# A transform-and-MLP kernel: the transforms end 16 ticks sooner, and one more block of tokens takes the seven-product form

## The chip, the cores and the metric

The kernel runs on one core of a Trainium2 chip. The metric is the device time of one execution in microseconds, given as the median of several runs. Its five engines appear as PE (TensorE matmuls; PEld is its weight load), DVE (VectorE), ACT (ScalarE), POOL (GpSimd) and SP (SyncE, which here only issues DMAs).

## What is computed

```python
# x: 4 x 3008 x 256
X = np.fft.rfft(x, axis=1)
Yr = Xr @ w_r - Xi @ w_i + b_r
Yi = Xr @ w_i + Xi @ w_r + b_i
Yr = np.sign(Yr) * np.maximum(np.abs(Yr) - 0.01, 0.0)     # Yi likewise
y = np.fft.irfft(Yr + 1j * Yi, n=3008, axis=1)
h = y.reshape(12032, 256) @ w_in                          # 2048 wide
out = (h * (1.0 / (1.0 + np.exp(-h)))) @ w_out            # 256 wide
```

A Fourier transform along the sequence, a complex 256 x 256 product with soft thresholding, the inverse transform, and then an MLP with SiLU over 12032 tokens. Matrices are kept as a high and a low part, so a product is three matmuls.

## The kernel before

The MLP is the frame. Its 12032 tokens are 24 blocks of 512 (the last has 256), and each block takes 16 **ticks**, one for each 128 of the 2048 hidden columns. In a plain tick t TensorE does six matmuls of 512 columns (`mlp1`, line 599), then what the table `fill` holds for that tick, then four pairs of accumulating matmuls (`mlp2`, lines 757 and 761) for the hidden columns of two ticks ago, then what `fill` holds for t + 0.5. ScalarE does SiLU and the rounding to the high part (lines 606, 615), VectorE the low part (line 616). Blocks 10 to 22, the set `FAST`, compute the first product in the seven-product form of Strassen and Winograd: for two ticks 21 matmuls of 256 columns (`fast_product`, line 680) instead of 12 of 512, with sums of the moving matrix on GpSimd (`fast_moving`) and sums of the products on VectorE (`fast_more`, `fast_two`). The weights' sums (`fast_weights`) and buffers for this need the memory that the transforms hold, so `swap_pools` frees it after the last transform step.

The transforms of batches 1 to 3 stand in `fill`, tick by tick. (Batch 0 and the first stage of batch 1 run ahead of tick 0.) Each has
- 16 **pieces** of the first stage for batches 2 and 3: `stack_split` splits an input tile into high and low (ScalarE line 283, VectorE line 284) two ticks or so ahead of `stack_product` (two matmuls, line 293), whose results ScalarE and VectorE add (lines 294, 295). The tile comes by a DMA from GpSimd's queue.
- 15 **steps** (`u3_step(b, u, 0)`): the second stage for pair u of frequencies (`s2_3`: eight matmuls, line 390; ScalarE lines 398, 399, 401; VectorE lines 400, 402, 403), the split of an earlier result into zh and zl (`split_z`, lines 447, 448), and the inverse for a still earlier one (`i1`: six matmuls, line 462, copied by ScalarE in line 466 and stored).
- 12 **mixes** (`u3_step(b, u, 1)`, `mix3`): three products of six matmuls (line 415). The first is copied to q by ScalarE (line 421), and GpSimd adds the biases to it (lines 422, 423). The other two fill the two halves of a second bank, which VectorE adds to q in the deferred `shrink` (line 434, four times; then lines 437 and 438 for the threshold). `shrink` is issued ahead of the next tick or half tick.

Steps, mixes and pieces take their banks of PSUM by turns from two (`bank`), so each takes the bank that the last but one used and waits for its readers. `i2` and `i2_ends` (lines 524, 531) turn a block into the MLP's layout, at half ticks where a tick already has work.

The order comes from a planner loop in the last part of the kernel. It goes through the ticks from 24 on, gives each at most one of piece, mix and step, leaves out the first tick of a block (`boundary`), and adds the turnings that are due. In before it ends at tick 148, in block 9.

Of the kernel before, what the change touches and what calls it, by code (L numbers as in the profile page):

```python
# [33 lines left out]

STACKED = 2

FAST = range(10, 23)

X_BUFS = [0, 1, 2, 3, 4, 5, 6, 0, 1, 2, 3, 4, 0, 2, 1, 0]
BLOCKS = [(c, min(BLK, NT - c)) for c in range(0, NT, BLK)]  # L40
# [109 lines left out]
def spectral_mlp_kernel(ctx: ExitStack, tc: tile.TileContext, x, w_r, w_i, b_r, b_i, w_in, w_out, c1, c2, c3, c4, c3f, c5, out):  # L150
    nc = tc.nc
# [8 lines left out]
    x_sb = [tf.tile([128, 4 * D], F32, name=f"x_sb{i}") for i in range(2)]  # L160
    c4_sb = cst.tile([120, 2 * (NP + RR)], F32, name="c4_sb")
    c5_sb = tf.tile([128, 128], F32R, name="c5_sb")
# [9 lines left out]
    state = {"prologue": True, "fast": False, "d": 0, "xy": 0}  # L172
    tl = None

    def bank(name):

        state["d"] += 1
        tag, bufs = f"d{state['d'] % 2}", 1
        if state["prologue"]:
            tag, bufs = ((f"d{state['d'] // 4 % 2}", 1), ("acc", 4), ("h", 2), ("acc", 4))[state["d"] % 4]  # L180
        if state["fast"]:
            tag = "d1"
        return ps.tile([128, 512], F32, tag=tag, bufs=bufs, name=name)
# [30 lines left out]

    def x_load_twice(b, q):

        t = x_sb[q % 2]
        if b == STACKED and q < 2:
            nc.gpsimd.memset(t[32:64, :], 0.0)
        h, g = divmod(q, 8)  # L220
        v = x[b].rearrange("(n h j) d -> n h (j d)", h=2, j=NJ)[:, h, g * 4 * D:(g + 1) * 4 * D]
        for p in (0, 64):
            nc.gpsimd.dma_start(out=t[p:p + RR, :], in_=v)
        return t
# [143 lines left out]
    def mix3_weights():  # L368
        t = tf.tile([128, 2, 2 * D], F32, tag="s1o", bufs=2, name="w32")
        nc.sync.dma_start(out=t[:, :, 0:D], in_=w_r.rearrange("(e p) d -> p e d", p=128))  # L370
        nc.sync.dma_start(out=t[:, :, D:2 * D], in_=w_i.rearrange("(e p) d -> p e d", p=128))
        for i, v in enumerate((b_r, b_i)):
            nc.sync.dma_start(out=bias[:, i, :], in_=v.unsqueeze(0).to_broadcast([128, D]))
        yield
        ds = []
        for op in (ALU.subtract, ALU.add):
            ds.append(tf.tile([128, 2, D], F32, tag="i1o", bufs=2, name="w32d"))
            nc.vector.tensor_tensor(out=ds[-1], in0=t[:, :, D:2 * D], in1=t[:, :, 0:D], op=op)
        yield
        for d, dst in zip(ds, (wi, ws)):  # L380
            nc.scalar.copy(dst[0], d)
            nc.vector.tensor_sub(dst[1], d, dst[0])
# [95 lines left out]
    def pieces(c0, n):  # L478

        c = c0  # L480
        while c < c0 + n:
            b, q = divmod(c, S)
            v = next(v for v in PLACES[b] if v[0] <= q < v[0] + v[1])
            p0 = q - v[0]
            m = min(v[1] - p0, c0 + n - c)
            yield c - c0, b, v, p0, m
            c += m
# [47 lines left out]

    def stage_bank(name, i):

        if i < 3 or state["fast"]:
            return bank(name)
        return ps.tile([128, 512], F32, tag="h", bufs=2, name=name)  # L540

    def i2(i, e):

        c0, n = BLOCKS[i]
        if e == 0:
            v = "ab"[i > 0] if i < 3 else "ab"[(i + 1) % 2]
            xt[i] = tuple(sb.tile([128, 2, BLK], F32R, tag=f"xt{v}{k}", bufs=1, name=f"xt{k}") for k in range(2))
        whole = [v for v in pieces(c0, n) if v[4] == v[2][1]]
        p = stage_bank("i2", i)
        for o, b, place, _, m in whole:  # L550
            i2_columns(p[:, o:o + m], e, b, place)
        q = slice(whole[0][0], whole[-1][0] + whole[-1][4])
        if i in FAST and e == 0:
            xf[i] = tl.tile([128, 2, BLK], F32, tag="xf", bufs=1, name="xf")
        split_x(i, p[:, q], (slice(None), e, q))

    def split_x(i, v, q):
        h, l = xt[i]
        nc.scalar.copy(h[q], v)
        if i in FAST:  # L560
            nc.scalar.copy(xf[i][q], v)
# [59 lines left out]
    xf, th, tw, fast = {}, {}, {}, []  # L621
# [118 lines left out]
    def mlp2(i, f, t):  # L740
# [31 lines left out]
        if i == LAST:  # L772
            (nc.vector.tensor_copy if t % 2 else nc.scalar.copy)(out=o, in_=a[:, 0:D])
        elif i in FAST and t < 2:
            w = sb.tile([128, 512], F32, tag="g", bufs=3, name="ow")
# [72 lines left out]
    with tc.manual_schedule():  # L848
# [156 lines left out]
        def at(t, fn, *args):  # L1005
            fill.setdefault(t, []).append((fn, args))

        taken = {9, 25} | set(range(33, len(ticks), NFF))

        def put(t, fn, *args):  # L1010

            while t in taken:
                t += 1
            taken.add(t)
            at(t, fn, *args)
            return t

        def last_stage(i, first):

            at(first - 2, i2_load, i)  # L1020
            put(first, i2, i, 0)
            put(first + 2, i2, i, 1)
            at(first + 2, i2_load, i, True)
            return put(first + 4, i2_ends, i)

        for k, fn in enumerate(((i2, 1, 0), (i2, 1, 1), (i2_ends, 1))):
            put(1 + 2 * k, *fn)
        last_stage(2, 25)
        for t, n in enumerate(W_GO):
            at(t, w_go, n)  # L1030
        at(0, x_ahead)
        for i in range(2):
            put(5, s1_later, 7, i)
        for t in (11, 35):
            at(t, x_ahead)
        at(30, nc.gpsimd.dma_start, c5_sb, c5)
        m3 = mix3_weights()
        for t in (16, 22, 23):
            at(t, next, m3, None)
# [1 line left out]
        steps = []  # L1041
# [2 lines left out]
                steps.extend((b, u, half) for half in range(2 if 0 < u <= NU else 1))  # L1044
        pieces_left = [(b, q) for b in range(STACKED, NB) for q in range(16)]
        turned = []
        for i in range(3, FAST[0]):
            at(16 * i - 15, i2_load, i)
            begins = any(v[1] and v[2][0] == 0 for v in pieces(*BLOCKS[i]))
            turned.extend((16 * i - (3 if k == 2 and begins else 13), 16 * i - 7 + 2 * k, fn)  # L1050
                          for k, fn in enumerate(((i2, i, 0), (i2, i, 1), (i2_ends, i))))
        stacked, last, begun = {1: 18}, 24, set()
        ended = {}
        done, t, since = 37, 24, 0
        while steps or turned:
            boundary = t % NFF == 1 and t > 32
            stage = None
            if not boundary and t not in taken:
                b = steps[0][0] if steps else NB
                ready = b in stacked and t >= stacked[b] + (4 if b > 1 else 0)  # L1060
                apart = 2 + (ready and b > 1 and len(pieces_left) % 2)
                if pieces_left and t >= done + apart and pieces_left[0][0] <= b + 1:
                    stage = "piece"
                elif ready:
                    stage = "mix" if steps[0][2] else "step"
            more = None
            if turned and t >= turned[0][0] and t >= since + 2 and not (boundary and t < turned[0][1]):
                if stage in ("mix", None) or t >= turned[0][1]:
                    more = turned.pop(0)[2]
                    since = t  # L1070
            if stage == "piece":
                at(max(t - 2, done), stack_split, *pieces_left[0])
                at(t, stack_product, *pieces_left[0])
                done = t
                if pieces_left.pop(0)[1] == 15:
                    stacked[max(stacked) + 1] = t
            elif stage:
                if b not in begun:
                    begun.add(b)
                    for k in range(2):  # L1080
                        at(t - 2 + k, u_load, b, k)
                at(t, u3_step, *steps.pop(0))
                last = t
                ended[b] = t
            if more:
                at(t + 0.5 * (stage is not None), *more)
                if more[0] is i2_ends:
                    at(t - 2, i2_load, more[1], True)
            t += 1
        assert ended[1] < 16 * 5 - 5 and ended[2] < 16 * 11 - 15 and ended[3] < 16 * 17 - 15  # L1090
        assert all(16 * i > t for t, v in fill.items() for fn, (i, *_) in [(v[0][0], v[0][1] or (99,))] if fn is i2_ends)

        for i in range(FAST[0], len(BLOCKS)):
            if i in FAST:
                first = max(16 * i - 13, last + 1)
                t = last_stage(i, first)
# [13 lines left out]
        for q in range(NFF // 2):  # L1110
            steps = fast_weights(q)
# [20 lines left out]
        for t in range(len(ticks) + 1):  # L1132
            i, f = ticks[t] if t < len(ticks) else (LAST, None)
# [4 lines left out]
            if i in FAST:  # L1138
                q = t - first_fast
# [62 lines left out]
```

## Time and profile before

| | |
|---|---|
| median of 3 runs | 1337.1 us (1334.11 to 1339.39) |
| profiled execution | 1336.09 us |
| its span | 1334.2 us |
| TensorE busy | 1320.7 us (99%), 8437 matmuls |
| VectorE, ScalarE, GpSimd busy | 907.5 (68%), 811.4 (61%), 215.0 (16%) us |
| chain that ended last | PE 93%, DMA 3%, DVE 1%, ACT 1% |

The busy time of matmuls is a union of modelled spans, which overlap: a matmul of 512 columns is shown with about 396 ns and one of 256 with 281 ns, but in a row they start closer together. What a matmul costs TensorE is read from the starts in the timeline. The chain follows the work that ended last back from the end of the program; it runs almost wholly through TensorE. The MLP's lines 757, 680, 599 and 761 hold 73% of it.

### The profile page before, as it was taken

To read this page: it belongs to the slowest core of one execution; us is meant where nothing else is said; L and a number is where in the kernel's file an instruction comes from. 1 tells how busy PE (TensorE), PEld (TensorE's weight loads), DVE (VectorE), ACT (ScalarE), POOL (GpSimd) and SP (SyncE) were. 2 spreads that over 40 slices of the span, in tenths; PEclk is the share of its full clock that TensorE was granted. 3 is DMA by queue.
4 is the path that set the end of the run, shared out by engine and by line. 5 is a ranking of instruction groups with operands and counts; after the bars stand their busy time and mean duration, and the time that the engine had idled before them with its cause. 6 is when DMAs were issued, how large, how long until landed. Compare 5 with 4: busy or idle time off the path is not lost.

```text
span 1334.2 us, 22834 instructions
## 1 busy us (share of the span) xinstructions
PE 1320.7 (99%) x8437; PEld 1182.2 (89%) x8437; DVE 907.5 (68%) x1742; ACT 811.4 (61%) x1712; POOL 215.0 (16%) x322
## 2 busy tenths in 40 slices
PE   8999999999999999999999999999999999999998
PEld 4977888888888888889988999999999999999998
DVE  3767747877767777566658766666666666666663
ACT  5546555766767666555455666566656665666555
POOL 2001002222212122111202111121112111211100
PEclk9999999999999999999999999999999999999999
DMA  8875414454455443424220111011001110110000
GB/s 267 267 218 185 142 55 116 107 153 114 120 149 142 123 139 93 121 79 124 77 69 3 45 32 29 3 32 32 21 3 46 32 32 2 32 31 14 3 23 25
DMA packets 76124, 110.00 MB, mean 82 GB/s; under 512 B 8854, under 2 KB 54798, under 8 KB 76014
## 3 DMA queue, kind: packets, MB, share of 16 engines
q1 hardware_dynamic: 61895, 79.17, 20.4%
q0 software_dynamic: 10544, 25.68, 7.6%
q10 hardware_dynamic: 3575, 3.70, 0.9%
q8 instruction: 67, 1.10, 0.3%
q14 instruction: 43, 0.35, 0.1%
HBM read 71.03 MB, written 37.49 MB: 81 GB/s over the span
## 4 chain that ended last, share of the span: by engine, by line
PE 93%; DMA 3%; DVE 1%; ACT 1%; issue 0%; SPq 0%; POOL 0%; ACTq 0%; DVEq 0%
PE acc L757 25%; PE h L680 19%; PE h L599 16%; PE acc L761 13%; PE mix L415 6%; PE s L390 2%; PE i L462 2%; PE mix L354 2%; PE i L531 2%; PE i2e L531 2%; PE s L293 1%; DMA scr<-i1o 1%; DMA scr<-s1o 1%; PE acc L752 1%; PE i L459 1%; PE s L333 1%
## 5 line engine op out<-in xcount | busy, mean ns | idle before, releaser
L757 PE MATMUL acc<-wout,gh 128*128 128x512 f32 x1472 | 539.8, 396 | 0.6 <-ACT gh L615 0.6
L761 PE MATMUL acc<-wout,gl 128*128 128x256 f32 x1472 | 413.6, 281 | 0.5 <-DVE gl L616 0.5
L757 PEld LDWEIGHTS acc<-wout,gh 128*128 128x128 f32 x1472 | 277.9, 189 | 48.5 <-ACT gh L615 0.8
L761 PEld LDWEIGHTS acc<-wout,gl 128*128 128x128 f32 x1472 | 277.1, 188 | 4.9 <-DVE gl L616 1.6
L599 PE MATMUL h<-xt,win 128*128 128x512 f32 (+1 forms) x1056 | 265.9, 387 | 0.0
L599 PEld LDWEIGHTS h<-xt,win 128*128 128x128 f32 x1056 | 181.4, 188 | 36.1 <-DVE xt L563 0.4
L606 ACT ACTIVATE g<-h 128x512 f32<-128x512 f32 (+1 forms) x177 | 102.1, 577 | 134.2 <-PE h L599 132.2
L728 DVE TENSOR_TENSOR gl<-gp,gh 128x512 fp32r<-128x512 f32 x208 | 148.5, 714 | 31.8 <-ACT gh L727 31.8
L718 ACT ACTIVATE gp<-gp 128x256 f32<-128x256 f32 x104 | 43.4, 417 | 176.8 <-DVE gp L715 176.8
L616 DVE TENSOR_TENSOR gl<-g,gh 128x512 fp32r<-128x512 f32 (+1 forms) x177 | 117.5, 664 | 49.1 <-ACT gh L615 47.6
L727 ACT CAST gh<-gp 128x512 fp32r<-128x512 f32 x208 | 128.9, 620 | 6.6
L680 PE MATMUL h<-xt,win 128*128 128x256 f32 x624 | 108.9, 283 | 0.2 <-DVE gp L715 0.2
L615 ACT CAST gh<-g 128x512 fp32r<-128x512 f32 (+1 forms) x177 | 106.1, 600 | 1.0
L720 DVE TENSOR_TENSOR gp<-h,u 128x256 f32<-128x256 f32 x104 | 44.2, 425 | 78.8 <-ACT gp L719 78.8
L680 PEld LDWEIGHTS h<-xt,win 128*128 128x128 f32 x624 | 88.6, 189 | 5.1 <-DVE gp L715 0.7
L434 DVE TENSOR_TENSOR y<-q,mix 64x256 f32<-64x256 f32 x144 | 60.3, 419 | 46.9 <-PE mix L415 41.2
L680 PE MATMUL h<-th,sw_h 128*128 128x256 f32 x312 | 91.3, 292 | 0.0
L680 PE MATMUL h<-th,sw_l 128*128 128x256 f32 x312 | 88.4, 283 | 0.0
L680 PE MATMUL h<-tl,sw_h 128*128 128x256 f32 x312 | 87.7, 281 | 0.0
L422 POOL TENSOR_TENSOR q<-q,bias 128x256 f32<-128x256 f32 x36 | 28.1, 780 | 356.3 <-ACT q L421 356.3
L715 DVE TENSOR_TENSOR gp<-h,u 128x256 f32<-128x256 f32 x104 | 44.1, 424 | 54.8 <-PE h L680 54.5
L726 ACT ACTIVATE gp<-gp 128x512 f32<-128x512 f32 x104 | 66.4, 639 | 0.0
(175 smaller groups left out, 2431.6 us busy)
## 6 DMA issues: line engine op xcount, KB each, us to landing
a<-scr SPq DMA_DIRECT2D x48, 256.0 KB
x_sb<-in_x_dram POOLq DMA_DIRECT2D x64, 188.0 KB, 3.7
gin<-scr SPq DMA_DIRECT2D x48, 192.0 KB
t<-in_c_dram POOLq DMA_DIRECT2D x36, 256.0 KB, 3.5
scr<-i1o SPq DMA_DIRECT2D x36, 256.0 KB
t<-in_c_dram SPq DMA_DIRECT2D x48, 128.0 KB
scr<-s1o SPq DMA_DIRECT2D x32, 192.0 KB
scr<-s1o SPq DMA_DIRECT2D x13, 384.0 KB
```

What stands on the lines that cost most here:

```text
L415: nc.tensor.matmul(out=out, lhsT=x_[:, e, c, :], rhs=m[:, e, :], start=(n == 0), stop=(n == 5))
L434: nc.vector.tensor_tensor(out=y[64 * i:64 * i + 64, r, :], in0=q[rows, i, :], in1=pv[rows, i, :], op=op,)
L599: nc.tensor.matmul(out=p[:, :n], lhsT=w[:, e, f * 128:(f + 1) * 128], rhs=v[:, e, :n], start=(m == 0), stop=(m == 5),)
L606: nc.scalar.activation(out=g[:, q], in_=p[:, q], func=ACTF.Silu)
L615: nc.scalar.copy(gh[:, q], g[:, q])
L616: nc.vector.tensor_sub(gl[:, q], g[:, q], gh[:, q])
L680: nc.tensor.matmul(out=p, lhsT=w[j], rhs=m[k], start=(begins and n == 0), stop=(n == 2), skip_group_check=True,)
L726: nc.scalar.activation(out=v, in_=v, func=ACTF.Silu)
L727: nc.scalar.copy(h, v)
L728: nc.vector.tensor_sub(l, v, h)
L757: nc.tensor.matmul(out=a, lhsT=gh[:, q], rhs=wout[:, f].rearrange("p a c -> p (a c)"), start=begins, stop=False,)
L761: nc.tensor.matmul(out=a[:, D:2 * D], lhsT=gl[:, q], rhs=wout[:, f, 0, :], start=False, stop=ends,)
```

## The change

Block 9 joins `FAST`, so the transforms have to be done and the pools swapped ahead of it, 16 ticks sooner. To that end the planner's rules are altered: pieces of batch 2 start at tick 26 instead of 39, one every fourth tick at first (the first three share one input buffer, since the other holds half an output of block 0 until tick 33); block 2's turning goes by the planner; and a mix may share its tick with the step behind it, which then stands at t + 0.5. That is so for 14 ticks: 63, 64, 66 (batch 1), 72, 85, 96 (batch 2), 115, 116, 119, 120, 123, 124, 127 and 128 (batch 3). The last steps stand at ticks 67, 109 and 132 (before: 73, 119 and 148).

```diff
-FAST = range(10, 23)
+FAST = range(9, 23)
 ...
-        t = x_sb[q % 2]
-        if b == STACKED and q < 2:
+        t = x_sb[0 if b == STACKED and q < 3 else q % 2]
+        if b == STACKED and q in (0, 3):
             nc.gpsimd.memset(t[32:64, :], 0.0)
 ...
-        if i < 3 or state["fast"]:
+        if i < 2 or state["fast"]:
             return bank(name)
         return ps.tile([128, 512], F32, tag="h", bufs=2, name=name)
 ...
-        last_stage(2, 25)
+        at(23, i2_load, 2)
+        at(24, i2_load, 2, True)
 ...
-        for t in (11, 35):
+        for t in (11, 36):
             at(t, x_ahead)
-        at(30, nc.gpsimd.dma_start, c5_sb, c5)
+        at(12, nc.gpsimd.dma_start, c5_sb, c5)
 ...
-        for i in range(3, FAST[0]):
-            at(16 * i - 15, i2_load, i)
+        for i in range(2, FAST[0]):
+            if i > 2:
+                at(16 * i - 15, i2_load, i)
             begins = any(v[1] and v[2][0] == 0 for v in pieces(*BLOCKS[i]))
-            turned.extend((16 * i - (3 if k == 2 and begins else 13), 16 * i - 7 + 2 * k, fn)
+            turned.extend((25 if i == 2 else 16 * i - (3 if k == 2 and begins else 13), 16 * i - 7 + 2 * k, fn)
                           for k, fn in enumerate(((i2, i, 0), (i2, i, 1), (i2_ends, i))))
 ...
-        done, t, since = 37, 24, 0
+        done, t, since = 22, 24, 0
         while steps or turned:
             boundary = t % NFF == 1 and t > 32
             stage = None
-            if not boundary and t not in taken:
+            double = False
+            if (not boundary or steps and steps[0][2]) and t not in taken:
 ...
-                if pieces_left and t >= done + apart and pieces_left[0][0] <= b + 1:
+                if not boundary and pieces_left and t >= (done + 4 if len(pieces_left) > 29 else max(38 * (len(pieces_left) == 29), done + apart)) and pieces_left[0][0] <= b + 1:
                     stage = "piece"
                 elif ready:
                     stage = "mix" if steps[0][2] else "step"
+                    double = stage == "mix" and not boundary and len(steps) > 1 and (b == 3 and steps[0][1] % 3 or b == 2 and steps[0][1] % 4 == 1 or b == 1 and 2 in stacked)
 ...
-                if stage in ("mix", None) or t >= turned[0][1]:
+                if stage in ("mix", None) and not double or t >= turned[0][1]:
 ...
                 at(t, u3_step, *steps.pop(0))
+                if double:
+                    at(t + 0.5, u3_step, *steps.pop(0))
 ...
             if more:
                 at(t + 0.5 * (stage is not None), *more)
-                if more[0] is i2_ends:
+                if more[0] is i2_ends and more[1] > 2:
                     at(t - 2, i2_load, more[1], True)
```

The first place is VectorE at the end of batch 1. In before it does, from the last mix of the batch (tick 71) on: the sums and threshold of `shrink` (lines 434, 437, 438), a turning (line 563), the MLP's split (616), zl (448), and then the split of an input piece (284).

```order
L616 TENSOR_TENSOR gl<-g,gh 128x512
L434 TENSOR_TENSOR y<-q,mix 64x256 x4
L437 TENSOR_SCALAR q<-y 128x512
L438 TENSOR_TENSOR y<-y,q 128x512
L563 TENSOR_TENSOR xt_3767<-i_3935,xt_3766 128x376
L616 TENSOR_TENSOR gl<-g,gh 128x512
L448 TENSOR_TENSOR zl<-y,zh 128x512
L284 TENSOR_TENSOR sx<-x_sb_72,sx 47x1024
```

The same place now, from the block's output sums (line 780, tick 65) on:

```order
L780 TENSOR_TENSOR o<-acc,o 128x256 x4
L616 TENSOR_TENSOR gl<-g,gh 128x512
L284 TENSOR_TENSOR sx<-x_sb_72,sx 47x1024
L434 TENSOR_TENSOR y<-q,mix 64x256 x4
L437 TENSOR_SCALAR q<-y 128x512
L438 TENSOR_TENSOR y<-y,q 128x512
L448 TENSOR_TENSOR zl<-y,zh 128x512
```

The split of the input piece moved ahead of the sums, and zl follows the threshold with nothing between.

The second place is ScalarE in batch 3, one mix (copy of q, line 421) with the step behind it and the next mix. In before the step has a tick of its own, so the MLP's cast and SiLU of that tick (615, 606) stand between q and the step's xh (398), here with a turning (559) too:

```order
L421 COPY q<-mix 128x256
L559 CAST xt_6778<-i_6780 128x235
L615 CAST gh<-g 128x512
L606 ACTIVATE g<-h 128x512
L398 CAST xh<-s_6804 128x2x256
L399 COPY xs<-s_6804 128x256
L401 CAST xh<-xs 128x2x128
L447 CAST zh<-y 128x512
L466 COPY i1o<-i_6822 128x512
L615 CAST gh<-g 128x512
L606 ACTIVATE g<-h 128x512
L421 COPY q<-mix 128x256
```

The same place now, at a doubled tick (119 and 120):

```order
L421 COPY q<-mix 128x256
L398 CAST xh<-s_6423 128x2x256
L399 COPY xs<-s_6423 128x256
L401 CAST xh<-xs 128x2x128
L447 CAST zh<-y 128x512
L466 COPY i1o<-i_6441 128x512
L615 CAST gh<-g 128x512
L606 ACTIVATE g<-h 128x512
L421 COPY q<-mix 128x256
```

Between two mixes the work of one tick, one cast and one SiLU, has gone; on TensorE that is one `mlp1` and one `mlp2`.

## Rows read from the trace of the kernel before

**Rows 1.** The page's first part: span; busy us of each engine, share, instructions.
```profile
span 1334.2 us, 22834 instructions
PE 1320.7 (99%) x8437; PEld 1182.2 (89%) x8437; DVE 907.5 (68%) x1742; ACT 811.4 (61%) x1712; POOL 215.0 (16%) x322
```

**Rows 2.** Windows: length, busy us of PE, PEld, DVE, ACT, POOL; PEclk, DMA, GB/s.
```profile
175.00:727.00 552.00, 551.60 (x3286) 486.71 (x3285) 394.18 (x714) 342.12 (x680) 112.78 (x177) 1.00 0.40 108
727.00:1304.00 577.00, 576.81 (x4059) 540.08 (x4058) 389.37 (x811) 358.10 (x811) 89.83 (x120) 1.00 0.09 24
```

**Rows 3.** Timeline of TensorE, two plain ticks: start, us, engine, line, operation.
```profile
604.05 1.57 PE L599 MATMUL h<-xt,win 128*128 128x512 f32 x6
...
606.86 1.55 PE L599 MATMUL h<-xt,win 128*128 128x512 f32 x6
```

**Rows 4.** Timeline of TensorE, two pairs of ticks of a fast block.
```profile
900.04 0.53 PE L680 MATMUL h<-xt,win 128*128 128x256 f32 x3
...
905.36 0.53 PE L680 MATMUL h<-xt,win 128*128 128x256 f32 x3
```

**Rows 5.** Timeline of TensorE: a step, a plain tick's work, a mix.
```profile
618.08 1.05 PE L390 MATMUL s<-t,a 128*128 128x128 f32 x8
618.88 0.36 PE L462 MATMUL i<-zh,t 128*128 128x256 f32 x1
...
619.68 0.40 PE L757 MATMUL acc<-wout,gh 128*128 128x512 f32 x1
...
621.08 1.56 PE L599 MATMUL h<-xt,win 128*128 128x512 f32 x6
622.48 0.40 PE L415 MATMUL mix<-wr,xh 128*128 128x256 f32 x2
...
624.51 0.28 PE L415 MATMUL mix<-ws,xl 128*128 128x256 f32 x1
```

**Rows 6.** Timeline of ScalarE behind the step of rows 5.
```profile
620.83 0.62 ACT L447 CAST zh<-y 128x512 fp32r<-128x512 f32 x1
621.35 0.58 ACT L466 COPY i1o<-i 128x512 f32<-128x512 f32 x1
```

**Rows 7.** Timeline of VectorE behind the step and the mix of rows 5.
```profile
620.40 0.68 DVE L402 TENSOR_TENSOR xl<-s,xh 128x512 fp32r<-128x512 f32 x1
...
621.48 0.69 DVE L448 TENSOR_TENSOR zl<-y,zh 128x512 fp32r<-128x512 f32 x1
...
624.90 1.72 DVE L434 TENSOR_TENSOR y<-q,mix 64x256 f32<-64x256 f32 x4 [1.73 <-PE mix L415]
```

**Rows 8.** Timelines of TensorE and VectorE: a mix and a split in one tick.
```profile
229.99 0.28 PE L415 MATMUL mix<-ws,xl 128*128 128x256 f32 x1
...
230.27 1.74 DVE L284 TENSOR_TENSOR sx<-x_sb,sx 47x1024 fp32r<-47x1024 f32 x1 [1.63 <-ACT sx L283]
232.04 1.72 DVE L434 TENSOR_TENSOR y<-q,mix 64x256 f32<-64x256 f32 x4
...
234.26 0.69 DVE L438 TENSOR_TENSOR y<-y,q 128x512 f32<-128x512 f32 x1
```

**Rows 9.** Timelines of TensorE, ScalarE and VectorE: a mix whose q is late.
```profile
393.97 0.28 PE L415 MATMUL mix<-ws,xl 128*128 128x256 f32 x1
...
393.72 0.38 ACT L421 COPY q<-mix 128x256 f32<-128x256 f32 x1
...
394.95 1.72 DVE L434 TENSOR_TENSOR y<-q,mix 64x256 f32<-64x256 f32 x4 [0.89 <-POOL q L422]
```

**Rows 10.** Timeline of TensorE: the matmuls behind its longest wait.
```profile
97.33 1.32 PE L524 MATMUL i<-c_sb,gin 96*128 96x94 f32 x10 [2.67 <-DMA gin<-scr]
```

**Rows 11.** Windows behind that wait (PEclk is the third column from the end).
```profile
98.80:100.00 1.20, 1.20 (x2) 0.34 (x1) 0.65 (x1) 0.44 (x1) 0.00 (x0) 0.50 0.92 176
100.00:102.20 2.20, 2.20 (x7) 1.42 (x6) 0.24 (x1) 1.06 (x3) 0.00 (x0) 0.53 0.96 365
102.20:103.00 0.80, 0.80 (x8) 0.69 (x7) 0.00 (x0) 0.49 (x1) 0.00 (x0) 1.00 0.84 338
```

More of the change, by code (lines that the diff above doesn't have):

```diff
@@ L1086, in spectral_mlp_kernel @@
                 at(t + 0.5 * (stage is not None), *more)
-                if more[0] is i2_ends:
+                if more[0] is i2_ends and more[1] > 2:
                     at(t - 2, i2_load, more[1], True)
             t += 1
-        assert ended[1] < 16 * 5 - 5 and ended[2] < 16 * 11 - 15 and ended[3] < 16 * 17 - 15
+        assert ended[1] < 75 and ended[2] < 16 * 11 - 15 and ended[3] < 16 * 17 - 15
         assert all(16 * i > t for t, v in fill.items() for fn, (i, *_) in [(v[0][0], v[0][1] or (99,))] if fn is i2_ends)
```

## The prediction

> **What bounds the kernel now.** I read the page first: TensorE is busy for 1320.7 us of a span of 1334.2 us [rows 1]. A busy share alone doesn't say that TensorE works at its pace, so I read the windows next: from 175 to 727 us, where the transforms run beside the MLP, it is busy for 551.6 of 552 us, and from 727 to 1304 us for 576.8 of 577, at full clock [rows 2]. Last came its timeline: a plain tick (six matmuls of 512 columns, then four pairs of 512 and 256) starts 2.81 us after the one before it [rows 3], the same to the hundredth wherever nothing else is in the tick. So behind the first 130 us the time is the sum of TensorE's issue times, and hardly any wait is left to remove. VectorE (394 us) and ScalarE (342 us) are busy for 71% and 62% of the 552 us [rows 2]. A change can win here by fewer columns on TensorE, and it loses whatever new wait it puts in front of a matmul. Both are in this change.
>
> **What it removes.** Block 9 goes from the plain first product to the seven-product form. A plain pair of ticks takes 2 x 2.81 = 5.62 us [rows 3]; a pair in a fast block starts 5.32 us after the last [rows 4] (900.04 to 905.36), with 21 matmuls of 256 columns instead of 12 of 512. That is 0.30 us a pair and 8 pairs: **2.4 us less**. Its extra VectorE and GpSimd work lies beside TensorE, as it does for the thirteen fast blocks of before, whose windows show no idle TensorE [rows 2]. The entry into the fast blocks, with the turning, the weights' sums and the change of pools, keeps its distance to the last step (steps end at 132 instead of 148, both 12 ticks ahead of the first fast tick), so its waits move with it. The output sums of block 9 for the first two token tiles go to GpSimd, as in the other fast blocks; SyncE then waits for them with nothing urgent behind. All transforms, pieces and turnings are the same work in number, only 16 ticks sooner. For VectorE that means about the same 394 us less 16 x 0.7 us of splits, in 552 - 45 = 507 us, some 76%: no new bound.
>
> **What it adds: waits inside the doubled ticks.** In 14 ticks a mix and the next step now share a tick. Between them stand only the four accumulating pairs. All relations come from one step and one mix of before [rows 5 to 7]. Call L the start of a mix's last matmul (624.51) and F the start of a step's first (618.08).
> The step's second product (inverse, line 462) takes the bank of the mix's second product, which VectorE reads in the four sums of `shrink`. They start at 624.90 and last 1.72 us, so the bank is free at L + 2.1. In a doubled tick TensorE wants it at L + 0.12 + 1.40 (accumulation, 619.68 to 621.08) + 0.80 (step, 618.08 to 618.88) = L + 2.32. That fits, by 0.2 us, and is at nothing in the ordinary doubled tick; its cover is a VectorE that comes to the sums at once.
>
> At **ticks 85.5 and 96.5** that cover is gone: the mix's tick also splits an input piece, and the split stands ahead of the sums on VectorE. The same order in before (mix and split in one tick) shows the sums at 232.04 for a mix whose last matmul began at 229.99, done at L + 3.77 [rows 8]. There TensorE came much later; now it waits 3.77 - 2.32 = 1.45 us, twice: **2.9 us**.
>
> At **tick 67** the tail of batch 1 folds. Its last mix is in tick 66, with a split behind it, the step that splits z in 66.5, and the last inverse already in 67; before, these were ticks 71, 72 and 73, and the split came behind z. As there, y is ready at 234.26 + 0.69, L + 4.96 [rows 8]. Then zh takes 0.62 us on ScalarE [rows 6] and zl 0.69 us on VectorE [rows 7]: L + 6.3. TensorE wants zh at L + 0.12 + 1.40 + 0.80 (the inverse before it, 618.88 to 619.68) + 1.40 (mlp, 621.08 to 622.48) = L + 3.72, and zl 0.2 later: **2.4 us**, in two waits of about 1.9 and 0.5.
>
> At **tick 73** a piece follows a doubled tick that had no inverse in it. Its second product takes the bank that the step's low parts are read from, free at 620.40 + 0.68 = F + 3.00 [rows 7]; TensorE wants it at F + 0.80 + 1.40 + 0.23 (one matmul of 512 columns, a sixth of 1.40) = F + 2.43: **0.6 us**.
>
> A doubled tick with an inverse, followed by a mix: the mix's second half takes the inverse's bank, which ScalarE has copied at 621.35 + 0.58 = F + 3.85 [rows 6]; TensorE wants it at F + 0.80 + 0.80 + 1.40 + 0.71 = F + 3.71 (0.71 for six of the mix's eighteen matmuls, which start within 2.03 us). That is 0.14 us at ticks 64, 86, 117, 120, 121, 124, 125 and 128: **1.1 us**. Where two doubled ticks follow one another the copy of q comes late. Such a case is in before [rows 9]: q copied at 393.72, a quarter of a microsecond before L instead of a whole one, and the sums done at 394.95 + 1.72, L + 2.7 instead of L + 2.1. Against L + 2.32 that is 0.4 us at tick 116.5, where the step before has no inverse and TensorE is early; at 120.5 and 124.5, where q is less late, 0.1 each: **0.6 us**.
>
> Waits together: 2.9 + 2.4 + 0.6 + 1.1 + 0.6 = 7.6 us. The first, second and third have their order in the built program and their durations in rows; the last two (1.7 us) are differences of a tenth between large numbers and may as well be 0 or 3. The earlier pieces (from tick 26, one every fourth tick in one buffer) I set at 0: their input is asked for at least two ticks ahead, as before, and ticks 24 to 37 have room on VectorE; the other side is a wait of up to about 1 us behind the sums of two neighbouring pieces. A gain there is excluded, since no wait was there. The moved table load (tick 12) and block 2's turning in one of the MLP's banks cost nothing that a row shows.
>
> **Sum.** -2.4 + 7.6 = +5.2 us against the profiled execution's 1336.09 us (span 1334.2 us and 1.9 around it): 1341.3. The median of the runs, 1337.1, is 1.0 above that execution, so I give **1342.3**.
>
> **Rivals.** First, the waits are not there, or mostly hidden: a release comes sooner than the analogous place of before shows, or an earlier wait takes up a later one. Then only the columns count: 1337.1 - 2.4 = 1334.7, and up to 1339.5 with under 5 us of waits. For it speaks that two terms are tenths; against it that the waits of 85.5, 96.5 and 67 are over a microsecond and rest on an order that the program fixes. Second, **the clock**, which ends slower. After the one wait of 2.67 us ahead of the matmuls at 97.33 [rows 10] the granted clock stands at 0.50, which is 1.2 GHz, and is back at 2.4 GHz from 102.2 on [rows 11]; (1.00 - 0.50) x 1.2 + (1.00 - 0.53) x 2.2 = 1.6 us lost. The wait at tick 67 is nearly as long, though in two parts and with matmuls up to it. If the clock falls there, +5.2 + 1.6 = +6.8 us, 1343.9, just beyond what counts as slower; the point from which it decides is a single wait of about the length of that one. The Trainium skill has the rule (TensorE: Matmul & The Clock Gate, section "HAM oscillation — how this bites in real kernels"): a wait for data between bursts can put the array back to half its clock, and half of the throttled time is then lost. By that rule the trace agrees at 97 us; it can't say whether a wait broken in two suffices. Third, the denser early ticks queue up on ScalarE and VectorE, a further 1 to 3 us: 1343 to 1345. That the change doesn't do what it says is ruled out: TensorE's list has 72 rows more, 8 pairs of 9.
>
> **How the numbers follow.** A measurement of this kernel can tell about 0.5%, 6.7 us, from no change. Forecast (waits of 5 to 9 us): 0.52, of which 0.12 lies over 6.7 us. Waits mostly hidden: 0.24, all within 0.5%. Clock: 0.15, slower. Early queues: 0.05, slower. Faster by over 0.5% would need some 4 us that no row shows: 0.04. So slower 0.12 + 0.15 + 0.05 = 0.32, same 0.40 + 0.24 = 0.64, faster 0.04. The range, 1335 to 1346, reaches from nearly all waits hidden to the clock's case with 2 us on top, and leaves out about 0.2.
>
> **What would show it.** TensorE's time lost against its pitch should stand at ticks 67 (line 462, released by VectorE's zl), 85.5 and 96.5 (line 462, by the sums of line 434) and 73 (line 293), and a pair of block 9 should take 5.3 us. If line 462 does not wait there, the second and third terms are wrong; if the granted clock drops near tick 67, the second rival holds; if waits stand in ticks 26 to 37, the third.

## The result, and the profile after

The changed kernel takes **1347.97 us** (median of 6 runs, 1344.93 to 1350.43) against 1336.28 us of the kernel before in the same session (6 runs, 1334.05 to 1339.39): a ratio of 1.0084, 95% interval 1.0069 to 1.0099. It is slower by 11.7 us, where 5.2 were forecast, and lies 2 us above the range. The page's first part after, which answers to [rows 1]:

```profile
span 1348.5 us, 23061 instructions
...
PE 1326.5 (98%) x8509; PEld 1185.8 (88%) x8509; DVE 926.0 (69%) x1780; ACT 816.2 (61%) x1734; POOL 223.0 (17%) x332
```

TensorE has 72 matmuls more, as it must (8 pairs of 9). The windows of the changed kernel (length; busy us of PE, PEld, DVE, ACT, POOL; clock, DMA share, GB/s), which answer to [rows 2]:

```profile
175.00:690.00 515.00, 507.46 (x3028) 444.66 (x3027) 378.62 (x680) 317.27 (x637) 114.28 (x178) 1.00 0.42 114
690.00:1317.00 627.00, 626.43 (x4397) 585.98 (x4396) 423.70 (x884) 388.50 (x877) 96.80 (x130) 1.00 0.09 23
```

Where TensorE was idle for 0.4 us beside the transforms, it is now idle for 7.5 us, and the modelled spans hide part of it. So I counted from the starts: for each two matmuls in a row, start to start less the usual distance of that line and shape (234 ns for line 599, 232 for 757, 119 for 761, 120 for lines 415 and 462), summed by tick. (For line 390 it is 111 ns, also where an inverse follows it at once and before shows 30; so the waits at such places, 85.5 and 96.5 among them, are counted 0.08 us too short each.) Tick 0 is the first matmul of line 599. It starts at 103.34 us in the profile of before and at 106.81 in that of the changed kernel (TensorE's timelines):

```profile
103.34 1.36 PE L599 MATMUL h<-xt,win 128*128 128x512 f32 x4
```
```profile
106.81 1.36 PE L599 MATMUL h<-xt,win 128*128 128x512 f32 x4
```

These 3.5 us are not the change's: its edits begin behind tick 0. The matmuls behind the wait of [rows 10] start at 99.34 us instead of 97.33, and the clock's low stretch behind them was longer; the windows show 3.4 us of it in before (first fence; in its third column from the end stands the granted clock) and 6.8 us after (second):

```profile
98.80:102.20 3.40, 3.40 (x8) 1.76 (x7) 0.89 (x2) 1.50 (x4) 0.00 (x0) 0.52 0.95 298
```
```profile
99.00:105.80 6.80, 6.46 (x19) 4.32 (x20) 0.89 (x2) 1.61 (x4) 0.00 (x0) 0.50 0.83 266
```

A second profile of the same changed kernel has no low stretch there and starts tick 0 at 100.08. Below I therefore compare the time **from tick 0 to the end of the span**: 1334.16 - 103.34 = 1230.8 us before and 1348.51 - 106.81 = 1241.7 us after, a difference of 10.9 us. By ticks:

| place | forecast, us | measured, us |
|---|---|---|
| distances without waits (block 9's pairs) | -2.4 | -2.64 |
| ticks 85.5 and 96.5 | 2.9 | 1.51 + 1.51 = 3.02 |
| tick 67 | 2.4 | 3.06 |
| tick 73 | 0.6 | 0.67 |
| mixes behind doubled ticks, late q (64, 86, 116, 117, 120, 121, 124, 125, 128) | 1.7 | 2.90 |
| ticks 31 and 34 | 0 | 0.47 + 0.92 = 1.39 |
| tick 108 | - | 0.66 |
| ticks 139 and 141 (entry of block 9; before: 0.54 at 157) | 0 | 0.57 + 1.03 - 0.54 = 1.06 |
| fast blocks (4.03, before 3.11) | 0 | 0.92 |
| waits of before that are gone (91, 109) | - | -0.53 |
| differences under 0.12 each | - | 0.37 |
| sum | +5.2 | +10.88 |

**The foreseen places.** Timeline of TensorE at tick 67 (start, us, engine, line, operation; in brackets the idle time and who ended it):

```profile
358.70 1.55 PE L599 MATMUL h<-xt,win 128*128 128x512 f32 x6
362.46 0.39 PE L462 MATMUL i<-zh,t 128*128 128x256 f32 x1 [2.21 <-ACT zh L447]
363.19 0.38 PE L462 MATMUL i<-zl,t 128*128 128x256 f32 x1 [0.34 <-DVE zl L448]
```

It is the wait of the forecast, line 462 for zh and then zl. VectorE and ScalarE show why it is longer, 3.06 us instead of 2.4 (L, the start of the mix's last matmul, is 356.47 here):

```profile
357.09 1.73 DVE L284 TENSOR_TENSOR sx<-x_sb,sx 47x1024 fp32r<-47x1024 f32 x1 [1.02 <-ACT sx L283]
358.86 1.72 DVE L434 TENSOR_TENSOR y<-q,mix 64x256 f32<-64x256 f32 x4
...
361.07 0.69 DVE L438 TENSOR_TENSOR y<-y,q 128x512 f32<-128x512 f32 x1
362.44 0.69 DVE L448 TENSOR_TENSOR zl<-y,zh 128x512 fp32r<-128x512 f32 x1 [0.68 <-ACT zh L447]
```
```profile
355.69 0.42 ACT L421 COPY q<-mix 128x256 f32<-128x256 f32 x1
355.95 1.12 ACT L283 CAST sx<-x_sb 111x1024 fp32r<-111x1024 f32 x1
361.79 0.62 ACT L447 CAST zh<-y 128x512 fp32r<-128x512 f32 x1 [4.73 <-DVE y L438]
```

VectorE's half of the split starts at L + 0.62 and not at L + 0.28 as in [rows 8], since ScalarE's half comes behind the copy of q: the row of line 283 ends at 357.07. At 85.5 the bank is free when the sums of line 434 end, 441.35 + 1.72 = 443.07; the trace calls the wait "issue", because it finds no event for it:

```profile
440.83 1.05 PE L390 MATMUL s<-t,a 128*128 128x128 f32 x8
443.17 0.36 PE L462 MATMUL i<-zh,t 128*128 128x256 f32 x1 [1.28 <-issue]
```
```profile
439.60 1.74 DVE L284 TENSOR_TENSOR sx<-x_sb,sx 47x1024 fp32r<-47x1024 f32 x1 [2.28 <-ACT sx L283]
441.35 1.72 DVE L434 TENSOR_TENSOR y<-q,mix 64x256 f32<-64x256 f32 x4
```

Tick 73 waits in line 293 for xl, 0.63 us and 0.07 behind it, against 0.6:

```profile
387.34 0.47 PE L293 MATMUL s<-sx,c_sb 111*128 111x512 f32 x1 [0.47 <-DVE xl L402]
```

**The places that were not foreseen.** TensorE's timeline shows a mix at tick 31, the accumulation at tick 34 (its first wait of two), and three places of the fast blocks:

```profile
207.92 0.51 PE L415 MATMUL mix<-wr,xh 128*128 128x256 f32 x2 [0.20 <-DVE s1o L295]
...
221.74 0.51 PE L757 MATMUL acc<-wout,gh 128*128 128x512 f32 x1 [0.17 <-DVE o L780]
...
681.64 0.38 PE L761 MATMUL acc<-wout,gl 128*128 128x256 f32 x1 [0.30 <-DVE gl L616]
...
688.27 0.38 PE L761 MATMUL acc<-wout,gl 128*128 128x256 f32 x1 [0.75 <-DVE gl L616]
...
760.00 1.51 PE L531 MATMUL i2e<-c_sb,gin 120*128 120x141 f32 x8 [0.34 <-DMA gin<-scr]
```

The rows at 681.64 and 688.27 are the MLP at ticks 139 and 141, where VectorE forms the weights' sums for the fast blocks; the last is the turning of block 11 (0.8 us with the two distances behind it). The brackets show less than was lost, as the matmul ahead is drawn past its own pace: between 687.12 and 688.27, a distance of 1.15 us, 0.92 are lost.

### The profile page after: what moved, and what is told of

Read it like the earlier page. It is cut to its first block, busy times and chain, and to the rows that moved or that the text cites. A ratio compares the mean times of both kernels' runs of the same rounds, so it can differ in the third digit from the quotient of the medians.

```text
span 1348.5 us, 23061 instructions
## 1 busy us (share of the span) xinstructions
PE 1326.5 (98%) x8509; PEld 1185.8 (88%) x8509; DVE 926.0 (69%) x1780; ACT 816.2 (61%) x1734; POOL 223.0 (17%) x332
## 4 chain that ended last, share of the span: by engine, by line
PE 88%; DMA 4%; DVE 2%; issue 2%; ACT 2%; POOL 0%; SPq 0%; ACTq 0%; DVEq 0%; POOLq 0%
PE acc L757 24%; PE h L680 19%; PE h L599 14%; PE acc L761 12%; PE mix L415 6%; PE s L390 2%; PE i L462 2%; PE mix L354 2%; PE i L531 2%; PE i2e L531 1%; PE s L293 1%; DMA scr<-i1o 1%; DMA w<-in_moe_w_in_dram 1%; DMA scr<-s1o 1%; PE acc L752 1%
## 5 line engine op out<-in xcount | busy, mean ns | idle before, releaser
L599 PE MATMUL h<-xt,win 128*128 128x512 f32 (+1 forms) x960 | 241.0, 386 | 0.0
L599 PEld LDWEIGHTS h<-xt,win 128*128 128x128 f32 x960 | 164.6, 188 | 32.0 <-DVE xt L563 0.4
L728 DVE TENSOR_TENSOR gl<-gp,gh 128x512 fp32r<-128x512 f32 x224 | 160.0, 714 | 34.1 <-ACT gh L727 34.1
L606 ACT ACTIVATE g<-h 128x512 f32<-128x512 f32 (+2 forms) x161 | 92.6, 576 | 91.1 <-PE h L599 89.1
L727 ACT CAST gh<-gp 128x512 fp32r<-128x512 f32 x224 | 138.9, 620 | 7.1
L616 DVE TENSOR_TENSOR gl<-g,gh 128x512 fp32r<-128x512 f32 (+2 forms) x161 | 105.9, 659 | 52.3 <-ACT gh L615 51.0
L680 PE MATMUL h<-xt,win 128*128 128x256 f32 x672 | 117.3, 283 | 0.2 <-DVE gp L715 0.2
L680 PEld LDWEIGHTS h<-xt,win 128*128 128x128 f32 x672 | 95.5, 189 | 5.2 <-DVE gp L715 0.4
L680 PE MATMUL h<-th,sw_h 128*128 128x256 f32 x336 | 98.3, 293 | 0.0
L615 ACT CAST gh<-g 128x512 fp32r<-128x512 f32 (+2 forms) x161 | 96.3, 599 | 1.0
L680 PE MATMUL h<-th,sw_l 128*128 128x256 f32 x336 | 95.2, 283 | 0.0
```

Source lines behind the costliest of these rows:

```text
L599: nc.tensor.matmul(out=p[:, :n], lhsT=w[:, e, f * 128:(f + 1) * 128], rhs=v[:, e, :n], start=(m == 0), stop=(m == 5),)
L606: nc.scalar.activation(out=g[:, q], in_=p[:, q], func=ACTF.Silu)
L615: nc.scalar.copy(gh[:, q], g[:, q])
L616: nc.vector.tensor_sub(gl[:, q], g[:, q], gh[:, q])
L680: nc.tensor.matmul(out=p, lhsT=w[j], rhs=m[k], start=(begins and n == 0), stop=(n == 2), skip_group_check=True,)
L727: nc.scalar.copy(h, v)
```

## The experiments

All are edits of the changed kernel. The table gives the time from tick 0 on, from one profile each, and the waits by place (us). Ratios are to the kernel before, with their interval; a dash stands where a kernel was run once.

| kernel | from tick 0 | 31, 34 | 67, 68 | 85, 96 | 116-128 | 139, 141 | fast blocks | ratio |
|---|---|---|---|---|---|---|---|---|
| before | 1230.8 | 0 | 0 | 0 | 0 | 0 | 3.1 | 1 |
| changed | 1241.7 | 1.4 | 3.1 | 3.0 | 2.4 | 1.6 | 4.0 | 1.0084 |
| changed, second profile | 1243.4 | 1.4 | 4.6 | 3.0 | 2.4 | 1.6 | 4.1 | 1.0088 (1.0069 to 1.0108) |
| block 9 plain | 1241.6 | 1.4 | 3.1 | 3.0 | 2.4 | 0 | 2.9 | 1.0088 (1.0072 to 1.0104) |
| early pieces only | 1233.6 | 1.4 | 0 | 0 | 0 | 0 | 3.0 | 1.0027 (1.0017 to 1.0037) |
| split behind | 1238.0 | 1.4 | 1.1 | 0 | 2.4 | 1.6 | 4.0 | 1.0062 (1.0048 to 1.0077) |
| swap at 67 | 1242.5 | 1.4 | 4.3 | 3.0 | 2.4 | 1.6 | 4.1 | - |
| block 9's output sums on VectorE | 1244.6 | 1.4 | 5.7 | 3.0 | 2.4 | 1.6 | 4.5 | - |
| inverse first | 1240.7 | 1.4 | 2.7 | 3.0 | 2.2 | 1.6 | 4.0 | - |
| moving sums on VectorE | 1242.7 | 1.4 | 5.7 | 3.0 | 2.4 | 0 | 4.4 | - |
| loads early | 1240.3 | 1.4 | 3.1 | 3.0 | 2.4 | 1.6 | 3.2 | - |
| first combination | 1235.2 | 1.4 | 1.1 | 0.4 | 2.2 | 0 | 4.7 | 1.0025 (1.0012 to 1.0038) |
| second combination | 1232.8 | 1.4 | 0 | 0 | 2.2 | 0 | 3.5 | 1.0020 (1.0008 to 1.0032) |

My theory was that the doubled ticks make the waits; the first rival, that block 9's fast form does.

**Block 9 plain.**

```diff
-FAST = range(9, 23)
+FAST = range(10, 23)
```

> Changed kernel with block 9 put back to the plain form; transforms still end at tick 132. Theory (the loss is made by the doubled and early ticks, block 9 itself gains): the trace keeps the waits of ticks 31, 34, 64, 67, 73, 85, 96, 108, 116 to 128 (about 10.5 us together), and a pair of block 9 takes 5.62 us again, so the time from tick 0 on is 1.0 to 2.6 us above the changed kernel's (the 2.6 us of columns are lost; up to 1.6 us of waits at the entry of the fast blocks and for the output sums may go with them): 10.5 to 13 us above the kernel before. Rival (the fast form of block 9 is what costs, by its entry, its sums on GpSimd or its heavier VectorE): the time falls below the changed kernel's, to less than 6 us above the kernel before.

The theory is right on the waits and wrong on the time. All waits of the transforms stay, to 0.02 us, and the kernel is 10.8 us above the one before, so the schedule alone makes the loss. But the time is not 1.0 us or more above the changed kernel's; it is the same (1241.6 to 1241.7). The 2.6 us that block 9 saves are taken back by the 1.6 us at 139 and 141 and by 1.1 us in the fast blocks.

**Early pieces only** (block 9 plain, no doubled tick).

```diff
-double = stage == "mix" and not boundary and ...
+double = False
```

> Changed kernel with block 9 plain and no doubled tick: of the change only the early pieces (from tick 26) stay; the transforms end at tick 144. Theory (the doubled ticks cost some 8 us, the early pieces 1.4): the waits of ticks 31 and 34 stay (0.47 and 0.92 us), those of 64, 67, 73, 85, 96, 108 and 115 to 128 are gone; the time from tick 0 on is 1 to 2.5 us above the kernel before. Rival (the sums and splits are crowded by the early schedule itself, doubled or not): waits of 4 us or more in all at ticks 37 to 132.

The theory's split holds: 31 and 34 stay as they were, the doubled ticks' waits are gone, and 1241.6 - 1233.6 = 7.9 us is what doubling costs on balance. The 2.8 us above before are more than the 1 to 2.5 expected: two new waits turn up, 0.84 us at tick 79 and 1.50 at tick 95. What makes them was not tested.

**The split behind the doubled tick.**

```diff
-at(max(t - 2, done), stack_split, *pieces_left[0])
+s = max(t - 2, done)
+at(s + 0.5 * (s in doubled), stack_split, *pieces_left[0])
```

> Changed kernel, with the split of an input piece moved behind the second half of a doubled tick (ticks 66, 85, 96), nothing else. Theory (the split stands on VectorE ahead of the shrink sums and of z): the waits of 85.5 and 96.5 (1.45 us each) and of 67 (2.97 us) all go; 5 to 6 us less than the changed kernel. Rival one (the bank is late for another cause, the late copy of q): 85 and 96 keep over 1 us each. Rival two (tick 67 waits because the last mix, the step that splits z and the inverse stand in a row, whatever the split does): 67 keeps over 2 us, and the gain is about 3 us.

The gain is 3.7 us, where 5 to 6 were expected. 85 and 96 are free of waits: the split ahead of the sums was their whole cause. Tick 67 falls from 3.1 to 1.1 us only, so rival two holds in part: mix, split of z and inverse in a row are 1.1 us too long even with VectorE free. And 1.4 us come back as the splits are now late for their pieces (0.37 us at tick 87, 1.00 at 98). TensorE at tick 67, and at tick 98, where line 293 waits for the split:

```profile
357.56 0.38 PE L462 MATMUL i<-zh,t 128*128 128x256 f32 x1 [0.30 <-ACT zh L447]
358.29 0.38 PE L462 MATMUL i<-zl,t 128*128 128x256 f32 x1 [0.34 <-DVE zl L448]
...
492.43 0.70 PE L293 MATMUL s<-sx,c_sb 111*128 111x512 f32 x2 [0.24 <-DVE sx L284]
```

**Piece and last step swapped.** In the planner's table the entries `stack_product(3, 0)` (68) and `u3_step(1, 14, 0)` (67) change places.

> Changed kernel, with the product of piece (3, 0) at tick 67 and batch 1's last step at tick 68, changed in places; the split stays in tick 66 ahead of the sums. Theory (zh and zl come too late by 3 us for an inverse one tick on): the wait at the last inverse goes whole, tick 67 loses 3.0 us of waiting and none over 0.3 us comes at 68; 85 and 96 keep 1.45 us each. Rival (the late y holds up the piece's own work on VectorE or its banks): a wait of 1 us or more stands at the piece's second product or at tick 69 in its place.

The theory falls, the rival holds: tick 67 still loses 2.8 us, now at the piece. The other 1.5 of the table's 4.3 us stand at tick 68, where the granted clock fell (0.50 from 364 to 366 us), and are not the swap's. The piece's second product takes the bank of the inverse in 66.5, and ScalarE, strictly in order, copies that bank (line 466) only behind zh, which waits for the late y:

```profile
358.95 0.47 PE L293 MATMUL s<-sx,c_sb 111*128 111x512 f32 x1 [0.44 <-DVE y L434]
361.18 0.50 PE L293 MATMUL s<-sx,c_sb 111*128 111x512 f32 x1 [1.76 <-ACT i1o L466]
```
```profile
360.02 0.62 ACT L447 CAST zh<-y 128x512 fp32r<-128x512 f32 x1 [4.73 <-DVE y L438]
360.55 0.58 ACT L466 COPY i1o<-i 128x512 f32<-128x512 f32 x1
```

**Block 9's output sums on VectorE.**

```diff
-elif i in FAST and t < 2:
+elif i in FAST[1:] and t < 2:
```

> Changed kernel, with block 9's output sums on VectorE instead of GpSimd. Theory (the load of block 10's tail waits on SyncE behind the store of block 9's output, which waits for GpSimd's sum): the wait of 0.8 us at tick 160 of the turning of block 10 goes, and the other waits of the fast blocks stay (about 3.1 us in all, as in the kernel before). Rival (the load is late for what GpSimd or the DMA queues do besides): the 0.8 us stay.

The wait stays (0.9 us at 759.43; by its tick it is block 11's turning, not block 10's as I called it). GpSimd's sum is not the cause. This profile showed another thing: 4.7 us at tick 67 and 1.0 at tick 68, in a stretch that this edit doesn't touch. Its granted clock stands at 0.50 from 360 to 364 us; this comes back below, with the second profile of the changed kernel.

**The inverse ahead of the split of z.** In `u3_step`, `i1(b, u - 3)` stands ahead of `split_z(b, u - 2)`.

> Changed kernel, with a step's inverse and its copy on ScalarE ahead of the split of z, so that ScalarE copies i1o before zh. Theory (the mix after a doubled tick waits for a bank that the copy of i1o frees): the 0.2 us at ticks 64, 86, 117, 121, 125 and 128 and part of those at 120 and 124 go, about 1.2 us in all. Price of the other side: zh and zl come later for the next inverse; if that counts, tick 67 and others grow by 0.5 us or more and the gain is lost.

A small part of it: the six mixes lose 0.06 us each and not 0.2. The rest of their wait stands at the mix's *first* product (0.11 to 0.15 us, line 415 behind line 599), whose bank was the step's. By the numbers of the forecast that bank is free at F + 3.00 and wanted at F + 0.80 + 0.80 + 1.40 = F + 3.00, a place with no room that I had not listed. Tick 108, a piece behind a step with an inverse, falls from 0.65 to 0.26 us, by the same copy of i1o.

**Block 9's moving sums on VectorE.**

```diff
+eng = nc.vector if i == FAST[0] else nc.gpsimd
-nc.gpsimd.tensor_sub(...)  (all 8 sums of fast_moving)
+eng.tensor_sub(...)
```

> Changed kernel, with the sums of block 9's moving side (fast_moving) on VectorE instead of GpSimd; the other blocks keep them on GpSimd. Theory (VectorE's sums of two operands take 0.71 to 1.23 us instead of 0.28 to 0.68 while GpSimd sums run beside them, and that makes gl late at ticks 139 and 141): the lines 628, 631 to 634 and 640 take 0.68, 0.29 and 0.68 us throughout, and the waits of 139 and 141 fall from 1.6 us to under 0.6, though VectorE has some 3 us more to do. Rival (VectorE has simply too much to do there): the waits of 139 to 143 grow to 2.5 us or more.

The theory holds: 139 and 141 fall from 1.6 us to nothing, though VectorE does eight sums more. In the 34 us around the entry VectorE is busy for the same time, 29.11 us with 62 instructions in the changed kernel and 29.07 with 72 here (663 to 697 and 660 to 694 us):

```profile
663.00:697.00 34.00, 32.95 (x172) 27.26 (x171) 29.11 (x62) 19.77 (x41) 7.65 (x8) 1.00 0.03 10
```
```profile
660.00:694.00 34.00, 33.70 (x181) 28.61 (x180) 29.07 (x72) 19.89 (x41) 0.00 (x0) 1.00 0.03 10
```

The timelines of VectorE and GpSimd in the changed kernel around tick 139, and then of VectorE in this one, show why:

```profile
672.21 0.68 DVE L640 TENSOR_TENSOR sw_l<-wd,sw_h 128x512 fp32r<-128x512 f32 x1
...
677.12 1.23 DVE L640 TENSOR_TENSOR sw_l<-wd,sw_h 128x512 fp32r<-128x512 f32 x1
678.28 1.23 DVE L628 TENSOR_TENSOR wf<-win,win 128x512 f32<-128x512 f32 x1
679.54 0.71 DVE L631 TENSOR_TENSOR wd<-wf 128x128 f32<-128x128 f32 x1
```
```profile
676.61 1.20 POOL L655 TENSOR_TENSOR td<-xf 128x256 f32<-128x256 f32 x1 [23.10 <-ACT rest L579]
677.88 1.07 POOL L657 TENSOR_TENSOR td<-xf,td 128x256 f32<-128x256 f32 x1
```
```profile
674.08 0.68 DVE L640 TENSOR_TENSOR sw_l<-wd,sw_h 128x512 fp32r<-128x512 f32 x1
674.68 0.68 DVE L628 TENSOR_TENSOR wf<-win,win 128x512 f32<-128x512 f32 x1
...
676.95 0.42 DVE L656 TENSOR_TENSOR td<-xf 128x256 f32<-128x256 f32 x1
```

The slowing itself is not new. VectorE in the kernel before, at the entry of block 10, where TensorE lost only 0.54 us:

```profile
708.83 1.23 DVE L640 TENSOR_TENSOR sw_l<-wd,sw_h 128x512 fp32r<-128x512 f32 x1
709.98 1.22 DVE L628 TENSOR_TENSOR wf<-win,win 128x512 f32<-128x512 f32 x1
```

New is where it falls. Just ahead of it VectorE splits 90 and 464 columns of block 9's turning (line 563), where block 10's had 6 and 78 there; the low part gl (line 616) behind the slow sums starts 4.2 us after the start of its tick (138) and not 3.1 as in before (154). That this is the whole of the 1.1 us is not shown.

**Block 11's boundary loads early.**

```diff
+for late in (False, True):
+    at(156 + late, i2_load, FAST[0] + 2, late)
```

> Changed kernel with block 11's boundary loads on SyncE at ticks 156 and 157, ahead of block 9's output stores, instead of 161 and 165. Theory (the loads stand in SyncE's queue behind the ten stores of block 9's output, whose last two tiles come a pair later in the fast form): the wait of 0.8 us for gin in the turning of block 11 goes, and nothing else changes. Rival (the load itself takes long, by its DMA queues or scratch rows): the 0.8 us stay.

The theory holds: no wait at line 531 is left, the fast blocks fall from 4.0 to 3.2 us, and the other waits of the table stay. (The rest of the 1.4 us by which the time is shorter lies in ticks 0 to 8, which differ by up to 0.7 us from profile to profile.) SyncE's queue in the changed kernel, and then here, where four of the eight loads (lines 499, 500) stand ahead of the stores (line 196):

```profile
748.53 4.71 SPq L196 DMA_DIRECT2D out_dram<-o  x8
753.33 0.32 SPq L499 DMA_DIRECT2D gin<-scr  x1
...
757.22 0.60 SPq L196 DMA_DIRECT2D out_dram<-o  x2
759.17 0.32 SPq L499 DMA_DIRECT2D gin<-scr  x1
```
```profile
707.12 0.32 SPq L499 DMA_DIRECT2D gin<-scr  x1
...
746.02 6.75 SPq L196 DMA_DIRECT2D out_dram<-o  x10
752.87 0.32 SPq L499 DMA_DIRECT2D gin<-scr  x1
```

**The changed kernel once more.**

> The changed kernel as it is, a second profile beside the two above. Theory (the wait at tick 67 is long enough that the clock falls in some executions and not in others): waits as in the first profile, and at tick 67 either 3.06 us with the granted clock at 1.00 throughout, or some 4.7 us and 1.0 us more at tick 68 with the clock at 0.50 from there to some 8 us later. Rival (the falls seen in two variants come from their edits): the clock stays at 1.00. The start of tick 0 lies between 101 and 107 us, by the clock in the 5 us ahead of it.

The same program, but behind the wait at tick 67 the clock fell: ticks 67 and 68 lose 3.6 and 1.0 us, less than the 4.7 and 1.0 expected for that case. Tick 0 starts at 100.08, just ahead of the range given. Windows of this second profile (two lines) and of the first one behind the same wait:

```profile
358.00:360.00 2.00, 2.00 (x8) 1.71 (x7) 0.69 (x1) 0.56 (x2) 0.00 (x0) 0.50 0.45 146
360.00:362.00 2.00, 2.00 (x7) 1.58 (x7) 0.00 (x0) 0.19 (x1) 0.00 (x0) 0.68 0.49 150
```
```profile
362.40:366.00 3.60, 3.20 (x18) 2.68 (x19) 2.08 (x3) 2.62 (x6) 0.00 (x0) 1.00 0.70 219
```
At 0.50 TensorE runs at 1.2 GHz instead of 2.4. Ticks 67 and 68 then cost 4.6 to 5.7 us instead of 3.1 (4.3 with the swap, whose order there is another). Of the eight profiles with 2 us or more of waiting at tick 67 the clock fell in four (this one, the swap, and the two with sums on VectorE) and stayed in four; of the four with 1.1 us or less there it fell in none. Such counts make the wait a likely cause and do not prove it.

**The combinations.** The first: splits of 85 and 96 a tick sooner and that of 66 behind; the inverse first; block 9's output and moving sums on VectorE.

> Changed kernel with four edits: the splits of ticks 85 and 96 one tick sooner and that of 66 behind the doubled tick's second half; the inverse ahead of the split of z; block 9's output sums on VectorE; block 9's moving sums on VectorE. Theory (each removes its own wait): 85, 96: -3.0 us; 67: -1.9; mixes after doubled ticks: -1.2; 139 and 141: -1.0; turning of block 10: -0.8; together about 8 us less than the changed kernel from tick 0 on, which leaves some 3 us above the kernel before. Rival (a removed wait comes back behind the next release): under 4 us less.

6.5 us instead of 8: 85 stays free and 96 keeps 0.4, but the load of block 11 waits as before (1.1 us with what follows it), and the mixes keep most of theirs. The second puts the splits into the tick of the piece before (62, 84, 94), swaps 67 and 68, and moves the loads; the inverse first and block 9's moving sums on VectorE stay in it.

> Changed kernel with: the splits of ticks 66, 85 and 96 in the tick of the piece before (62, 84, 94); the product of piece (3, 0) and batch 1's last step changed in places (67, 68); the inverse ahead of the split of z; block 9's moving sums on VectorE; block 11's boundary loads at ticks 156 and 157. Theory: no wait of over 0.5 us is left at ticks 67, 68, 85, 96, 139, 141 nor in the turning of block 11; 31, 34, 73 and 116 keep their 2.7 us; from tick 0 on some 8.5 us less than the changed kernel, 2 to 3 us above the kernel before, so no difference that a measurement can tell. Rival (the last mix of batch 1 and the piece behind it are late whatever the split does): 67 and 68 keep over 1.5 us and the gain is under 7.

The waits are as expected: 8.9 us less than the first profile of the changed kernel, no wait at 67, 68, 85, 96, 139, 141, and the same 2.7 us at 31, 34, 73 and 116. Its window beside the transforms, the same as above for the changed kernel:

```profile
175.00:690.00 515.00, 513.26 (x3079) 451.29 (x3078) 382.89 (x709) 321.69 (x646) 106.75 (x170) 1.00 0.43 114
```

The swap, which alone left a wait of 2.8 us at tick 67, works here, since the split no longer holds up y and the copy of i1o no longer stands behind zh. At 1.0020 (1.0008 to 1.0032) it is still 0.2% slower than the kernel before. No version beat that one: from tick 0 on it loses 4.6 us more than before to waits, against the 2.6 us that block 9 saves (1232.8 - 1230.8 = 2.0).

## Why the prediction went wrong

**What was right.** The sign and the mechanism: columns saved in block 9 (-2.4 forecast, -2.6 measured) against waits in the doubled ticks, at the lines that the forecast named. The terms of 85.5, 96.5 and tick 73 were right to 0.2 us each, and the split experiment shows the cause of the first two. The first rival (waits hidden) is refuted by each of them.

**Terms mis-sized, 1.9 us** (0.66 + 1.20). Tick 67 was put at 2.4 us from [rows 8] and measured 3.06: VectorE's half of the split came 0.34 us later there, as it waits for ScalarE's half, and behind each wait here the next distance was about 0.1 us longer than usual (line 462: 0.22 us from 363.19 on instead of 0.12). The two small terms were put at 1.1 + 0.6 and measured 2.90: the forecast listed the mix's second bank and overlooked its first, which has no room either, and called its bound "0 or 3" itself.

**Steps set to nothing, 4.0 us** (1.39 + 0.66 + 1.06 + 0.92). "The earlier pieces I set at 0" was wrong: the other end, about 1 us, was nearer to the measured 1.4, so the third rival holds, but small (the kernel with early pieces only keeps these waits). Tick 108 (0.7) was not seen. "Its waits move with it", of the fast blocks' entry, was wrong: the distance to the last step is the same, but TensorE loses 1.1 us more there. VectorE's sums slow down beside GpSimd's as in before, and now fall nearer to a low part that TensorE waits for; with the moving sums on VectorE the wait is gone. "SyncE then waits for them with nothing urgent behind" was wrong as well: behind the stores stand the loads of block 11's boundary. (GpSimd's sums are not what holds them: with these on VectorE the wait stays.) The last two took back what block 9 gained, as the kernel with block 9 plain shows. With 0.37 us of small differences and 0.53 us of old waits gone, this is the whole of the 5.7 us by which the time from tick 0 on missed the forecast.

**The clock.** I gave it 0.15 as a rival. It is no either-or: the same program lost 1.5 us to it in one profile and nothing in another, and variants up to 2.7 us. It is not needed for the difference of the medians, 11.7 us: the interval of the ratio reaches from 9.2 to 13.2 us, which covers the 10.9 of the first profiles. Nor do the runs' mean granted clocks show more of it after the change: they average 0.998 over 17 runs of before and over 11 of the changed kernel. By the Trainium skill (TensorE: Matmul & The Clock Gate, section "HAM oscillation — how this bites in real kernels") a wait between bursts can put the array back to half its clock. The falls here stand behind a wait, which agrees; that the same wait sometimes has no effect is what the traces add.

**The range** had its upper end at the clock's case with 2 us on top, so it held no room for several steps at nothing to be wrong together.

## What to carry to other kernels

When an engine is full to the last tenth, work that is packed closer costs at each bank and each in-order queue it shares, also where every single cover seems to hold: list every bank that a moved matmul takes, with its margin, and give a margin under 0.2 us a price. "Its waits move with it" needs the neighbours too: what else runs on the engines that now stand beside it, and what stands behind its stores in a DMA queue. A wait that may drop the clock should be priced both ways in the forecast, not as a case of its own.

## What the runs showed of the hardware

VectorE's sums with two operands in SBUF took 1.23 us instead of 0.68 (512 columns), and 0.71 instead of 0.29 (128), while GpSimd's sums ran, those shown 1.07 to 1.20 us long; eight sums moved from GpSimd to VectorE (0.42 us each) left VectorE's busy time around them as it was. The Trainium skill (GPSIMD Engine Reference, section "1. Specifications") says that the two share their SBUF interfaces and contend where a VectorE instruction has two SBUF inputs; that section names no size; the trace agrees and gives one.

The clock's fall is not decided by the program alone: with the same instructions and the same wait it fell at tick 67 in the second profile of the changed kernel and not in the first. Ahead of tick 0 the low stretch was 6.8, 3.4 or 0 us long. The last is the second profile of the changed kernel, where the matmuls of line 524 wait 2.67 us, as long as in [rows 10], and the granted clock stays at 1.00:

```profile
95.74 1.32 PE L524 MATMUL i<-c_sb,gin 96*128 96x94 f32 x10 [2.67 <-DMA gin<-scr]
```

So this wait, from which the prediction took the price of its second rival, does not always cost it. What tells these executions apart stays open.
